# Attention and MoE block on one core: batches two to four in blocks of 256 and 320 rows, single-head score groups, spare products in a bank of their own

## The chip, the cores and the metric

The kernel runs on one core of a Trainium2 chip. The core has five engines with queues of their own: TensorE (PE, with its weight loads as PEld), VectorE (DVE), ScalarE (ACT), GpSimd (POOL) and SyncE (SP), which issues nearly all DMAs. The metric is device time in microseconds, as the median of several executions; a profiled execution gives the trace.

## The reference

Eight batches of eight heads go through attention whose weights are kept only near each row's maximum, and the result goes through a gated two-layer network. In short:

```
scores = q @ k.T / 8                                   # (8, 8, 576, 576), head size 64
keep   = scores >= rowmax(scores) - tau
attn   = exp(scores - rowmax) where keep, else 0
x      = (attn / (sum(attn) + 1e-9)) @ v               # heads side by side: (4608, 512)
h      = x @ w_in                                      # (4608, 2048)
out    = (h * sigmoid(h)) @ w_out                      # (4608, 512)
```

The weights `w_in` and `w_out` reach the kernel as 64-bit words.

## The kernel before, in words

**Visits.** The unit of attention is a visit: one pair of heads of one batch. Its rows are cut into tiles of 128 (numbers 0 to 3) and a tile 4 that holds the last 64 rows of both heads. `VISITS` names three kinds: "low" has tiles 0 and 1 (rows 0 to 255), "high" has tiles 2, 3 and 4 (320 rows), "all" has the five. Before, batch 0 is done as four low visits (0 to 3) and four high ones (4 to 7); batches 1 to 7 as four "all" visits each (8 to 35).

**A score group and its softmax.** For a tile of two heads, PE writes two score tiles `s` (there are two in all, pool "s") in one group that interleaves the heads (line 999). Then, per head: DVE takes the maximum (601) and the threshold (604), ACT the exponential (614), DVE masks and sums (621). Outside the low visits, the weights are split into two half-precision parts: ACT or POOL make the upper part (685, 687), POOL the lower (693, 694), and a DMA transposes both into a buffer `wT`. In the low visits ("direct") PE turns the weights in single precision (669) back into the score tile, and ACT copies them out (673).

**Dividing by the sum.** For batches below `UNDIVIDED` the weights stay undivided: the reciprocals are spread over the columns by PE (770), copied by ACT (835) and multiplied into the block on DVE (839, 844). From that batch on, ACT divides each tile's weights (636), after two tiny DVE instructions (628, 633).

**Query and key.** Each visit loads its pair's query and key (545), ACT gates the query (550), and, outside the low visits, ACT and POOL split both into two parts (561, 564).

**The network.** `moe(b, c0, n)` works on a block of n rows: 16 products groups `h` (891, 12 products each), tanh on ACT (898), two DVE instructions and an ACT copy (903, 908, 911), then 4 x 4 groups `o` (941), a copy out (953) and a store. Block (0,0), the first 256 rows of batch 0, is done in single precision (882, 933). Batches 1 to 7 are done in two blocks of 288 rows. A block needs the value products `a` (801, 809) of all four visits that cover its rows.

**The weights** are loaded in 32 chunks and rebuilt from their bits by ACT (401, 425), POOL (392, 428), DVE (404) and PE (417, for the maxima); later ACT and DVE split them (458, 461).

**What sets the order.** All operations are given to a planner (`Plan`) with a cost and a priority, most of them a place in the row of softmax tiles; tables such as `W_AT` and `Q_OFF` hold the places of weight chunks and loads. It lists them by its own costs, pool by pool, and the program is emitted in that order; each engine then runs its instructions strictly in it. PSUM holds the two `s` tiles and a pool of four banks ("bank") for everything else.

**Spare products.** `fill` puts products of no use (589) into gaps that the plan leaves on PE in its first 230 us, for 0.6 of each gap; `WARM` of them stand at the very start. Before, they write into the unused columns of the second bank of the score tile that was made last:

```
def products():
    for _ in range(n):
        nc.tensor.matmul(last_s[0][:, 1, 288:512], ones, wide, start=True, stop=True)
```

Of the kernel before, what the change touches and what calls it, by code (L numbers as in the profile page):

```python
# [20 lines left out]
P = 128  # L21
# [12 lines left out]
SEM = 50  # L34
# [17 lines left out]
class Plan:  # L52
# [134 lines left out]
    def fill(self, eng, until, least, each, make):  # L187

        end, out = 0.0, []
        for o in self.done:  # L190
            if o.eng == eng:
                n = int(FILL * (o.start - end) / each)
                if end < until and o.start - end > least and n > 0:
                    f = Op()
                    f.eng, f.occ, f.lat, f.name, f.fn, f.alloc, f.vs = eng, n * each, n * each, "fill", make(n), [], []
                    f.start, f.end, f.idx, f.prio, f.ready = end, end + n * each, o.idx, 0.0, 0.0
                    out.append(f)
                end = o.start + o.occ
        self.done = sorted(self.done + out, key=lambda o: (o.start, o.idx))
# [9 lines left out]
W_AT = (40.0, 24.01, 22.15, 61.37)  # L209
V_AT = 12.64  # L210
V_OFF = (-40.55, -32.27, -20.0, -3.3)
Q_OFF = (-7.69, -2.43, 1.82)
HIGH_AT = -3.91
W_STEP = (0.9, 0.83, 1.49, 0.77)
UNDIVIDED = 2
BIAS = 12 * math.log(2.0)
FILL = 0.6
FILL_UNTIL = 230.0e3
WARM = 60
# [10 lines left out]
def attention_moe(  # L230
# [48 lines left out]
    wide = ones[:, 0:1].to_broadcast([P, 224])  # L279
    ident = const.tile([P, P], F32, name="ident")  # L280
# [295 lines left out]
    last_s = [None]  # L576

    def new_s(nm):
        def make(slot):
            last_s[0] = ps_s.tile([P, 2, 512], F32, tag="s", name=f"s_{nm}")  # L580
            return last_s[0]

        return pl.value(f"s_{nm}", "s", make)

    def occupied(n):

        def products():
            for _ in range(n):
                nc.tensor.matmul(last_s[0][:, 1, 288:512], ones, wide, start=True, stop=True)  # L589

        return products

    def softmax(nm, u, v, parts, s, sums, direct=False):
# [59 lines left out]
        if direct:  # L653
            for h, i, r0, rows in parts:
                if (v, h) not in wT:
                    def make(slot, h=h):
                        full = sb.tile([P, 9, S], F16, tag="wT", name=f"wT_{v}_{h}", bufs=3)
                        full = full.rearrange("p j c -> p (j c)").bitcast(F32)[:, 0 : 5 * n]
                        return full.rearrange("p (j c) -> p j c", j=5)

                    wT[v, h] = pl.value(f"wT_{v}_{h}", "wT", make)
            ((h, i, r0, rows),) = parts
            out, c = wT[v, h], i * P - base

            def turned():
                flat = s.t.rearrange("p j c -> p (j c)")
                for k in range(5):
                    o = k * P if k < 4 else S - P
                    nc.tensor.transpose(flat[:, k * P : (k + 1) * P], w.t[:, o : o + P], ident)  # L669

            def kept():
                flat = s.t.rearrange("p j c -> p (j c)")
                nc.scalar.activation(
                    out.t[:, :, c : c + rows], flat[:, 0 : 5 * P].rearrange("p (k r) -> p k r", k=5), AF.Copy
                )
# [100 lines left out]
    def av(v, p, c0, n, u, rr):  # L776
# [3 lines left out]
        w2 = [wT[v, b * H + 2 * p + odd] for odd in range(2)]  # L780
        direct = kind == "low"
# [12 lines left out]
        def product():  # L794
            if rr is not None:
                spread(ps, c0, n, rr)
            if direct:
                for k in range(5):
                    r = slice(D, P) if k == 4 else slice(0, P)
                    for odd in range(2):  # L800
                        nc.tensor.matmul(
                            a.t[odd * D : (odd + 1) * D, :n], vt.t[r, odd, k, :], w2[odd].t[r, k, :],
                            start=(k == 0), stop=(k == 4),
                        )
                return
# [24 lines left out]
        op("PE", (3480 if direct else 1715 * k + 90) + more, (3650 if direct else 1715 * k + 260) + more, u - 500, product,  # L830
# [140 lines left out]
    warm = new_s("warm")  # L971
    op("PE", 9000, 9000, 10 * URGENT, occupied(WARM), [], [warm], name="warm")

# [4 lines left out]
    def visit(v, b, p, kind, u):  # L978
# [3 lines left out]
        direct = kind == "low"  # L982
# [20 lines left out]

        for i in tiles:
            if i < 4:
# [18 lines left out]
            cost = 1150 if direct else 1080 if i < 4 else 985  # L1024
            op("PE", cost, cost + 155, u, score, reads, ss, name=f"score{v}_{i}")
# [9 lines left out]
    for v, (b, p, kind) in enumerate(visits):  # L1035
        if p == 0 and b > 0:
            prepare_v(b, *((lambda p, o=o: u + 9 * p + o) for o in V_OFF[:2]), u + V_OFF[2],
                      lambda p: u + 9 * p + V_OFF[3])
        u = visit(v, b, p, kind, u + HIGH_AT) - HIGH_AT if kind == "high" else visit(v, b, p, kind, u)
        if p == NPAIR - 1:  # L1040
            if kind != "low":
# [3 lines left out]
            if kind == "low":  # L1045
# [4 lines left out]
    pl.fill("PE", FILL_UNTIL, 250.0, 95.0, occupied)  # L1050
# [50 lines left out]
```

## Time and profile before

| | us |
|---|---|
| median of 3 runs (1186.49 to 1189.03) | 1188.85 |
| profiled execution | 1183.31 |
| its span in the trace | 1181.4 |
| PE busy in the span | 1135.6 |
| DVE busy | 859.1 |
| ACT busy | 842.9 |
| POOL busy | 652.3 |
| first product of block (0,0), of (0,256), of batch 1's first block | 99.5, 201.2, 308.2 |
| last value product | about 1039 |

The span is the time between the first and last recorded instruction. A matmul's record reaches from its start to its result, so neighbours overlap, and a run of products is better read by the distance of their starts. A group of the page gives the source line, the engine, what is written and read, the count, busy time and the mean of one, and behind the second bar the idle time of the engine ahead of it and who ended that. In the waits view a line reads: who waited, for whom, total us, times, the longest.

### The profile page before, as it was taken

How to read it: one execution, taken by the hardware profiler on the slowest of the kernel's cores; microseconds unless marked ns; L12 is line 12 of the kernel's file. 1: busy time of each engine (PE TensorE's matmuls, PEld its weight loads, DVE VectorE, ACT ScalarE, POOL GpSimd, SP SyncE). 2: the span in 40 equal slices, each digit the busy share in tenths (PEclk: the TensorE clock that was granted, in tenths of full speed). 3: DMA queues.
4: the chain of work that ended last, by engine and by line, in shares of the span. 5: the costliest groups of instructions: out<-in, count | busy, mean ns of one | idle time of the engine just before them, and what ended most of it. 6: DMA issues, size and time to landing. Idle time of an engine off the chain costs nothing.

```text
span 1181.4 us, 27974 instructions
## 1 busy us (share of the span) xinstructions
PE 1135.6 (96%) x10212; PEld 893.8 (76%) x10212; DVE 859.1 (73%) x2412; ACT 842.9 (71%) x1529; POOL 652.3 (55%) x894
## 2 busy tenths in 40 slices
PE   8777899997899999999999999999999999999998
PEld 6555777775777777777777777777777777877777
DVE  4667899986887869687787878787887869541331
ACT  4776786875877878787887878787887878552341
POOL 0568798677667565666666465756666575400000
PEclk9999999999899999999999999999999999999999
DMA  8536577577677666775768576766766575600000
GB/s 328 165 115 166 113 176 173 108 123 151 120 121 144 109 135 125 132 139 110 136 117 151 103 140 116 141 109 128 136 120 127 95 135 95 107 6 21 11 11 21
DMA packets 352153, 141.17 MB, mean 119 GB/s; under 512 B 326416, under 2 KB 334608, under 8 KB 352016
## 3 DMA queue, kind: packets, MB, share of 16 engines
q1 hardware_dynamic: 352016, 139.38, 58.5%
q8 instruction: 81, 1.33, 0.5%
q14 instruction: 56, 0.46, 0.1%
HBM read 49.68 MB, written 9.44 MB: 50 GB/s over the span
## 4 chain that ended last, share of the span: by engine, by line
PE 83%; DVE 7%; POOL 4%; issue 3%; ACT 2%; DMA 2%; POOLq 0%; ACTq 0%; DVEq 0%
PE h L891 29%; PE o L941 29%; PE s L999 11%; PE a L809 9%; DVE w L621 2%; DMA wT<-hl 2%; PE s L589 2%; DVE sm L601 1%; POOL hl L693 1%; PE h L882 1%; PE s_warm L589 1%; PE s L669 1%; ACT w L614 1%; DVE wst L404 1%; POOL wst L428 0%
## 5 line engine op out<-in xcount | busy, mean ns | idle before, releaser
L941 PE MATMUL o<-gbuf,wst 128*128 128x288 f16 (+1 forms) x2880 | 371.2, 287 | 0.0
L891 PE MATMUL h<-x,wst 128*128 128x288 f16 (+1 forms) x2880 | 369.5, 287 | 0.4 <-DVE gbuf L911 0.4
L693 POOL TENSOR_TENSOR hl<-w,hl 128x512 f16<-128x512 f32 x272 | 321.0, 1180 | 84.1 <-ACT hl L685 73.3
L891 PEld LDWEIGHTS <-wst 128*128 128x128 f16 x2880 | 277.0, 98 | 80.2 <-issue 8.7
L941 PEld LDWEIGHTS <-wst 128*128 128x128 f16 x2880 | 275.8, 98 | 81.2 <-issue 10.4
L614 ACT ACTIVATE w<-s,sm 128x576 f32<-128x576 f32 x288 | 210.1, 739 | 76.3 <-DVE sm L601 45.1
L621 DVE SCALAR_TENSOR_TENSOR w<-s,sm,w 128x576 f32<-128x576 f32 x288 | 230.8, 814 | 45.5 <-ACT w L614 41.8
L601 DVE TENSOR_REDUCE sm<-s 128x1 f32<-128x576 f32 x288 | 208.3, 749 | 72.3 <-PE s L999 60.8
L687 POOL TENSOR_SCALAR hl<-w 128x576 f16<-128x576 f32 x136 | 91.7, 675 | 200.8 <-ACT w L636 167.1
L636 ACT ACTIVATE w<-w,sm 128x576 f32<-128x576 f32 x216 | 162.8, 772 | 53.4 <-DVE sm L633 31.0
L903 DVE SCALAR_TENSOR_TENSOR h<-th,h 128x288 f32<-128x288 f32 (+1 forms) x240 | 109.6, 458 | 69.2 <-ACT th L898 65.6
L898 ACT ACTIVATE th<-h,msc 128x288 f32<-128x288 f32 (+1 forms) x240 | 121.0, 504 | 21.6 <-PE h L891 19.1
L911 DVE SCALAR_TENSOR_TENSOR gbuf<-h,gbuf 128x288 f16<-128x288 f32 (+1 forms) x240 | 108.2, 454 | 36.5 <-ACT gbuf L908 36.1
L908 ACT ACTIVATE gbuf<-h 128x288 f16<-128x288 f32 (+1 forms) x240 | 97.8, 410 | 46.2 <-DVE h L903 45.6
L809 PE MATMUL a<-wT,v 128*64 128x288 f16 (+1 forms) x1680 | 110.7, 288 | 0.0
L685 ACT ACTIVATE hl<-w 128x576 f16<-128x576 f32 x136 | 92.5, 682 | 17.7 <-DMA wT<-hl 5.6
L809 PEld LDWEIGHTS <-v 128*64 128x64 f16 x1680 | 92.5, 110 | 13.3 <-issue 5.5
L999 PE MATMUL s<-khi,qhi 64*128 64x288 f32 (+1 forms) x544 | 88.2, 350 | 13.1 <-DVE w L621 12.6
L999 PEld LDWEIGHTS s<-khi,qhi 64*128 64x128 f32 (+1 forms) x544 | 49.9, 187 | 47.7 <-issue 42.5
L694 POOL TENSOR_TENSOR hl<-w,hl 128x64 f16<-128x64 f32 x272 | 85.7, 315 | 0.0
L953 ACT ACTIVATE ot<-o,msc 128x288 f32<-128x288 f32 (+1 forms) x60 | 29.7, 494 | 66.4 <-PE o L941 65.9
L999 PE MATMUL s<-klo,qhi 64*128 64x288 f32 (+1 forms) x544 | 67.9, 294 | 0.0
(95 smaller groups left out, 1172.8 us busy)
## 6 DMA issues: line engine op xcount, KB each, us to landing
qraw<-in_qT SPq DMA_DIRECT2D x36, 320.0 KB, 3.4
kraw<-in_kT SPq DMA_DIRECT2D x36, 288.0 KB, 3.0
vraw<-in_vL SPq DMA_DIRECT2D x32, 320.0 KB, 3.3
wst<-in_w_in SPq DMA_DIRECT2D x16, 512.0 KB, 6.4
out_t<-ot SPq DMA_DIRECT2D x56, 144.0 KB, 2.1
wT<-hl SPq DMA_TRANSPOSE x304, 3.3
wraw<-in_w_out SPq DMA_DIRECT2D x8, 512.0 KB, 4.7
wst<-in_w_out SPq DMA_DIRECT2D x8, 512.0 KB, 3.8
```

The costliest lines, as they stand in the source:

```text
L601: nc.vector.tensor_reduce(out=sm.t[:, 0:1], in_=s.t[:, :, :HALF], op=ALU.max, axis=AX.XY, negate=True)
L614: nc.scalar.activation(w.t.rearrange("p (j c) -> p j c", j=2), s.t[:, :, :HALF], AF.Exp, bias=sm.t[:, 0:1] if direct or sums is None else ...
L621: nc.vector.scalar_tensor_tensor(out=w3, in0=s.t[:, :, :HALF], scalar=sm.t[:, 1:2], in1=w3, op0=ALU.is_ge, op1=ALU.mult, accum_out=sm.t[:, ...
L636: nc.scalar.activation(w.t, w.t, AF.Copy, scale=sm.t[:, 5:6])
L693: nc.gpsimd.tensor_tensor(out=fl[:, 640:1152], in0=w.t[:, 0:512], in1=fl[:, 0:512], op=ALU.subtract)
L809: nc.tensor.matmul(a.t[odd * D : (odd + 1) * D, :n], vt.t[:, lo_v, odd, kv, :], w2[odd].t[:, kw, c0 - base : c0 - base + n], start=(k == 0 ...
L891: nc.tensor.matmul(ph.t[:, :n], wi(c, f, lo_w), xview(b, lo_x, c, c0, n), start=(j == 0), stop=(j == 11),)
L898: nc.scalar.activation(th.t[:, :n], ph.t[:, :n], AF.Tanh, scale=0.5 if whole else scale.t[:, 0:1])
L903: nc.vector.scalar_tensor_tensor(out=gwhole(g, n) if whole else ph.t[:, :n], in0=th.t[:, :n], scalar=1.0, in1=ph.t[:, :n], op0=ALU.add, op ...
L911: nc.vector.scalar_tensor_tensor(out=g.t[:, 1, :n], in0=ph.t[:, :n], scalar=2.0**-14, in1=g.t[:, 0, :n], op0=ALU.mult, op1=ALU.subtract,)
L941: nc.tensor.matmul(po.t[:, :n], wo(f, d, lo_w), gs[f].t[:, lo_g, :n], start=(f == 0 and j == 0), stop=(f == NF - 1 and j == 2),)
L999: nc.tensor.matmul(out[:, j, :HALF], q.t[rows, i * P : (i + 1) * P], k.t[rows, j * HALF : (j + 1) * HALF], start=(m == 0), stop=(m == len( ...
```

## The change

- `DIVIDED = 4`: batches 1 to 3 are also done as four low and four high visits, and their network in blocks of 256 and 320 rows. That makes 48 visits in place of 36: 0 to 7 are batch 0, 8 to 15 batch 1 (low, then high), 16 to 31 batches 2 and 3, and from 32 on "all" visits. Each visit loads, gates and splits its query and key, so 12 more of these. Only batch 0's low visits stay "direct".
- `UNDIVIDED = 1`: batch 1 divides its weights on ACT, and its spread reciprocals go.
- `SINGLE = 7`: in visits 0 to 6 each head of a 128-row tile has a score group and a place in the order of its own.
- In the low visits of batch 0 the two heads share one `wT` buffer (of three) where each had its own; their value product moves behind by `AV_AT`.
- Spare products write into a free bank of the pool of four, in the longest stretch of the gap in which one bank is free. `WARM` goes from 60 to 28. In the emitted program there are 100 in place of 348.
- An exponential of one column, right after the constant `ones` is set, makes ACT load its table at the start.
- All tables of places are set anew.

```diff
-    def fill(self, eng, until, least, each, make):
+    def fill(self, eng, until, least, each, pool, make):
...
+        def free(a, b):
+
+            best = (0.0, a, None)
+            for slot, uses in taken.items():
+                t = a
+                for start, stop in [*uses, (b, b)]:
+                    if stop >= a and t < b:
+                        best = max(best, (min(start, b) - t, t, slot), key=lambda q: q[0])
+                        t = max(t, stop)
+            return best
...
-W_AT = (40.0, 24.01, 22.15, 61.37)
+W_AT = (47.67, 22.01, 23.98, 99.13)
...
-UNDIVIDED = 2
+UNDIVIDED = 1
...
+SINGLE = 7
+DIVIDED = 4
+AV_AT = 13.6
...
-WARM = 60
+WARM = 28
...
+    table = const.tile([P, 1], F32, name="table")
+    nc.scalar.activation(table, ones[:, 0:1], AF.Exp)
...
     def occupied(n):
+
+        spare = bank("spare")

         def products():
             for _ in range(n):
-                nc.tensor.matmul(last_s[0][:, 1, 288:512], ones, wide, start=True, stop=True)
-
-        return products
+                nc.tensor.matmul(spare.t[:, 0:224], ones, wide, start=True, stop=True)
+
+        return products, spare
...
-        direct = kind == "low"
+        direct = kind == "low" and b == 0
...
-    visits = [(0, p, kind) for kind in ("low", "high") for p in range(NPAIR)]
-    visits += [(b, p, "all") for b in range(1, B) for p in range(NPAIR)]
...
+    visits = [
+        (b, p, kind) for b in range(B) for kind in (("low", "high") if b < DIVIDED else ("all",)) for p in range(NPAIR)
+    ]
...
         for i in tiles:
+            if i < 4 and v < SINGLE:
+                for r in range(2):
+                    s = new_s(f"{v}_{r}{i}")
+
+                    def score(s=s, i=i, r=r):
+                        for m in range(len(products)):
+                            for j in range(2):
+                                product(s.t, i, m, j, r)
+
+                    op("PE", cost(i), cost(i) + 155, u, score, reads, [s], name=f"score{v}_{r}{i}")
+                    softmax(f"{v}_{r}{i}", u, v, [(ha + r, i, 0, P)], s, sums, direct)
+                    u += 1
+                continue
```

Where it moves instructions. On PE, in the first visit, before (`s_0_00` is visit 0, head 0, tile 0; `s_0_10` the other head; `kraw`, `qraw` key and query):

```order
L589 MATMUL s_warm_129<-ones_80 128x224
L999 MATMUL s_0_00_224<-kraw_0_190,qraw_0_192 128x288
L999 MATMUL s_0_10_225<-kraw_0_190,qraw_0_192 128x288
L999 MATMUL s_0_00_224<-kraw_0_190,qraw_0_192 128x288
L999 MATMUL s_0_10_225<-kraw_0_190,qraw_0_192 128x288
L589 LDWEIGHTS ones_80
L589 MATMUL s_0_10_225<-ones_80 128x224
```

The heads stand interleaved, and the spare products behind them write into `s_0_10`. The same visit's second tile now (line 1022 is the score product, 691 the turn, 609 the spare products):

```order
L609 LDWEIGHTS ones_80
L609 MATMUL spare_232<-ones_80 128x224
L1022 MATMUL s_0_01_244<-kraw_0_160,qraw_0_162 128x288 x2
L691 MATMUL s_0_10_189<-ident_84,w32_0_10_221 128x128 x5
L609 LDWEIGHTS ones_80
L609 MATMUL spare_256<-ones_80 128x224
```

Head 0's scores of tile 1 stand ahead of head 1's turn of tile 0, and the spare products have a tile of their own. On ACT, at the end of batch 0's second block, before (`ot_0_256_3` is the copy out of that block's last columns; `w32_11_03` the exponential of visit 11, tile 3; `hl` a half copy; `khi`, `qhi` halves of key and query):

```order
L953 ACTIVATE ot_0_256_3_3860<-o_0_256_3_3580,msc_0_98 128x320
L614 ACTIVATE w32_11_03_3878<-s_11_03_3846,sm_11_03_3865 128x576
L614 ACTIVATE w32_11_13_3880<-s_11_13_3847,sm_11_13_3871 128x576
L685 ACTIVATE hl_11_03_3884<-w32_11_03_3878 128x576
L685 ACTIVATE hl_11_13_3895<-w32_11_13_3880 128x576
L561 ACTIVATE khi_13_3899<-kraw_13_3529 128x576
L561 ACTIVATE qhi_13_3902<-qraw_13_3550 128x640
```

Batch 1's first tanh stands 28 rows behind that copy. Now, around the same copy (line 975; 920 is the tanh, 930 the network's upper half, 659 the division, 838 the block's upper half):

```order
L920 ACTIVATE th_1_0_1_3561<-h_1_0_1_3509,msc_1_104 128x256
L659 ACTIVATE w32_14_04_3507<-w32_14_04_3507,sm_14_04_3501 128x576
L930 ACTIVATE gbuf_61<-h_1_0_1_3509 128x256
L838 ACTIVATE x16_1_2272<-a_1_1_256_3531 128x320
L535 ACTIVATE v16_2_1_3589<-vraw_2_1_2123,v2_s2_107 128x640
L637 ACTIVATE w32_15_02_3614<-s_15_02_3573,sm_15_02_3608 128x576
L975 ACTIVATE ot_0_256_3_3633<-o_0_256_3_3212,msc_0_100 128x320
```

Batch 1's second tanh now stands ahead of batch 0's last copy out; its first is 13 rows ahead.

More of the change, by code (lines that the diff above doesn't have):

```diff
@@ L185, in run @@
         return max(o.end for o in done)
-    def fill(self, eng, until, least, each, make):
+    def fill(self, eng, until, least, each, pool, make):
+        taken = {}
+        for o in self.done:
+            for x in o.alloc:
+                if x.pool == pool:
+                    taken.setdefault(x.slot, []).append((o.start, x.freed + SEM))
+        def free(a, b):
[7 more added lines that the diff above has]
+            return best
         end, out = 0.0, []
@@ L191, in fill @@
             if o.eng == eng:
[L192 to L197, printed above, removed]
+                if end < until and o.start - end > least:
+                    length, at, slot = free(end, o.start)
+                    n = int(FILL * length / each)
+                    if n > 0:
+                        f = Op()
+                        f.eng, f.occ, f.lat, f.name, f.deps = eng, n * each, n * each, "fill", set()
+                        f.fn, x = make(n)
+                        x.slot = slot
+                        f.alloc, f.vs = [x], [x]
+                        f.start, f.end, f.idx, f.prio, f.ready = at, at + n * each, o.idx, 0.0, 0.0
+                        out.append(f)
                 end = o.start + o.occ
@@ L653, in softmax, with make @@
         if direct:
[L654 to L661, printed above, removed]
-            ((h, i, r0, rows),) = parts
-            out, c = wT[v, h], i * P - base
+            ((h, i, r0, rows),) = parts
+            if v not in wT:
+                def make(slot):
+                    full = sb.tile([P, 9, S], F16, tag="wT", name=f"wT_{v}", bufs=3)
+                    full = full.rearrange("p j c -> p (j c)").bitcast(F32)[:, 0 : 10 * n]
+                    return full.rearrange("p (h j c) -> p h j c", h=2, j=5)
+                wT[v] = pl.value(f"wT_{v}", "wT", make)
+            out, c = wT[v], i * P - base
             def turned():
@@ L673, in kept @@
                 nc.scalar.activation(
-                    out.t[:, :, c : c + rows], flat[:, 0 : 5 * P].rearrange("p (k r) -> p k r", k=5), AF.Copy
+                    out.t[:, h % 2, :, c : c + rows], flat[:, 0 : 5 * P].rearrange("p (k r) -> p k r", k=5), AF.Copy
                 )
@@ L779, in av @@
         a = bank(f"a_{b}_{p}_{c0}")
-        w2 = [wT[v, b * H + 2 * p + odd] for odd in range(2)]
-        direct = kind == "low"
+        direct = kind == "low" and b == 0
+        w2 = [wT[v]] if direct else [wT[v, b * H + 2 * p + odd] for odd in range(2)]
         vt = VRAW[0, p] if direct else V16[b, p]
@@ L981, in visit @@
         tiles, ranges = VISITS[kind]
-        direct = kind == "low"
+        direct = kind == "low" and b == 0
         ha = b * H + 2 * p
@@ L1035, in attention_moe @@
     for v, (b, p, kind) in enumerate(visits):
-        if p == 0 and b > 0:
+        if p == 0 and b > 0 and b not in VS:
             prepare_v(b, *((lambda p, o=o: u + 9 * p + o) for o in V_OFF[:2]), u + V_OFF[2],
                       lambda p: u + 9 * p + V_OFF[3])
-        u = visit(v, b, p, kind, u + HIGH_AT) - HIGH_AT if kind == "high" else visit(v, b, p, kind, u)
+        at = HIGH_AT if kind == "high" and b == 0 else 0.0
+        u = visit(v, b, p, kind, u + at) - at
         if p == NPAIR - 1:
-            if kind != "low":
+            if b not in MSC and v >= NPAIR:
                 moe_scales(b, u - 4)
@@ L1044, in attention_moe @@
                 moe(b, c0, n)
-            if kind == "low":
+            if v < NPAIR:
                 split(0, W_AT[2], W_STEP[2])
```

33 lines of the change are left out of this document (15 added, 18 removed).

## Prediction

> **What bounds the kernel now.** I began with the page: how long each engine is busy, and the chain that ended last.
>
> ```profile
> span 1181.4 us, 27974 instructions
> PE 1135.6 (96%) x10212; PEld 893.8 (76%) x10212; DVE 859.1 (73%) x2412; ACT 842.9 (71%) x1529; POOL 652.3 (55%) x894
> PE 83%; DVE 7%; POOL 4%; issue 3%; ACT 2%; DMA 2%; POOLq 0%; ACTq 0%; DVEq 0%
> ```
>
> PE carries the chain, but a busy PE need not be a useful one. So second came the table of windows (per window: PE, PEld, DVE, ACT and POOL busy, then the granted clock), cut where block (0,0) starts, where PE gets dense, where batch 0's last block is nearly done, and where batch 1's first block starts; the row from 140 to 250 repeats the middle of the dense stretch.
>
> ```profile
> 0.00:99.50 99.50, 79.15 (x636) 58.75 (x636) 58.69 (x142) 65.34 (x103) 45.96 (x63) 0.97 0.61 207
> 99.50:130.00 30.50, 22.71 (x165) 18.68 (x166) 23.84 (x57) 19.70 (x35) 26.09 (x39) 1.00 0.53 102
> 130.00:280.00 150.00, 145.22 (x1218) 111.84 (x1216) 134.77 (x303) 112.32 (x203) 118.16 (x175) 1.00 0.71 146
> 280.00:308.20 28.20, 19.63 (x212) 15.60 (x210) 21.08 (x54) 17.01 (x27) 17.89 (x30) 0.76 0.70 134
> 140.00:250.00 110.00, 106.05 (x864) 82.45 (x861) 105.30 (x236) 87.15 (x160) 89.53 (x127) 1.00 0.73 150
> 308.20:1040.00 731.80, 730.85 (x6862) 578.91 (x6861) 578.04 (x1766) 580.16 (x1060) 444.24 (x591) 1.00 0.67 123
> ```
>
> From 308.2 on PE never rests. Up to 99.5 nothing is the bound: ACT is busy 66%, DVE 59%, and much of PE's 79 us are spare products. From 140 to 250 DVE is (105.30 of 110, 96%). The time is therefore **the moment at which batch 1's first block starts, plus the PE work behind it**.
>
> That work I count by paces: a block of 192 products and a visit's two value products from the chain in order of time, and from the PE timeline a score group, from its start to the next row's: two heads together, and tile 4, whose products go one after another.
>
> ```profile
> 338.62 3.55 PE a L809 x56
> ...
> 1060.46 23.52 PE o L941 x192
> 342.10 0.53 PE L999 MATMUL s<-khi,qhi 64*128 64x288 f32 x4
> ...
> 343.09 4.58 PE L941 MATMUL o<-gbuf,wst 128*128 128x288 f16 x36
> ...
> 351.45 0.53 PE L999 MATMUL s<-khi,qhi 128*128 128x288 f32 x2
> ...
> 352.35 0.91 PE L941 MATMUL o<-gbuf,wst 128*128 128x288 f16 x6
> ```
>
> A pair costs 0.99, tile 4 0.90. Behind 308.2 stand 28 runs of 192 (658.6), 93 pairs (92.1), 24 tiles 4 (21.6) and 23 visits' value products (81.7): 854. The rest of the span is 1181.4 - 308.2 = 873, so 19 us are not used there, tail included. In front of 308.2 lies the loss. Its last piece is the hole between the two batches, in the PE timeline:
>
> ```profile
> 286.49 0.54 PE L999 MATMUL s<-khi,qhi 64*128 64x288 f32 x4
> ...
> 291.12 0.82 PE L999 MATMUL s<-khi,qhi 128*128 128x288 f32 x2 [3.57 <-DVE w L621]
> ...
> 295.83 0.81 PE L999 MATMUL s<-khi,qhi 64*128 64x288 f32 x3 [2.39 <-DVE w L621]
> ...
> 300.05 0.58 PE L999 MATMUL s<-khi,qhi 64*128 64x288 f32 x1 [2.45 <-DVE w L621]
> ...
> 308.23 1.52 PE L891 MATMUL h<-x,wst 128*128 128x288 f16 x11
> ```
>
> For 22 us PE has only scores and value products, waiting for the masks of the tiles before them: batch 1's block needs all 36 softmax tiles of its batch. The first piece is the low visits. One of them, all engines:
>
> ```profile
> 40.12 2.10 PE L999 MATMUL s<-kraw,qraw 64*128 64x288 f32 x8
> ...
> 42.53 1.53 PE L589 MATMUL s<-ones 128*128 128x224 bf16 x14
> ...
> 44.09 0.76 DVE L601 TENSOR_REDUCE sm<-s 128x1 f32<-128x576 f32 x1 [1.18 <-PE s L589]
> ...
> 50.41 0.70 ACT L673 ACTIVATE wT<-s 128x640 f32<-128x640 f32 x1 [1.78 <-PE s L589]
> ```
>
> L589 are spare products, written into the second head's score tile. Its maximum waits 1.18 us for them, its copy out 1.78 us; the pair takes 10 us.
>
> **The change, part by part.** *Spare products in their own bank.* The waits on them sum up in the waits of the first 130 us, and in ACT's groups up to 99.5:
>
> ```profile
> DVE sm L601 <- PE s L589: 10.3, 10, 1.9
> L673 ACT ACTIVATE wT<-s 128x640 f32<-128x640 f32 x16 | 11.3, 704 | 10.6 <-PE s L589 5.9 <-PE s L669 2.7 <-DVE v_s L307 2.0
> ```
>
> 10.3 + 5.9 = 16.2 us go; some of it is covered by weight work that is then late instead, so I take three quarters, 12. Bounds: 0 and 16.2.
>
> *Table load and 28 first products.* Now ACT loads its table when the first query has landed, and the first score starts behind sixty products:
>
> ```profile
> 1.06 8.80 PE s_warm L589 x60
> 5.22 1.28 ACT L550 ACT_TABLE_LOAD   x1 [5.22 <-DMA qraw<-in_qT]
> ...
> 6.51 0.83 ACT L550 ACTIVATE qraw<-qraw,gate 128x640 f32<-128x640 f32 x1
> ...
> 9.79 1.36 PE L999 MATMUL s<-kraw,qraw 64*128 64x288 f32 x8
> ```
>
> The gated query can be ready at 5.22 + 0.83 = 6.1 instead of 7.3, and 28 products at 8.80 / 60 us, or somewhat slower at the start, end near 6.3. First score 3.4 us earlier. Bounds: 1 and 3.4.
>
> *Single-head groups.* A head's group starts when its own bank is free, and the two heads of a low visit share one weight buffer, so that three visits can be under way (no wait on it stands in the views: nothing). PE pays for it: in the three high visits six pairs of 0.99 become twice 0.90 (+4.9 us), in the low ones a pair takes 1.36 to 2.10 today and would take about 2.1 (0 to +6). PE has room for 5 to 11 us there. What the earlier maxima bring I can't price by a row; I count nothing, and keep it as the low end.
>
> *Stage 1, to block (0,0)'s first product.* The order puts 4 more exponentials, 5 more half copies and 5 fewer weight copies of ACT ahead of it: 65.3 + 4.5 = 70 us of ACT. So 99.5 - 3.4 - 12 + 4.5 = **88**, ACT at 80%. Bounds: 78 (ACT at 90%) and 104 (only the added work).
>
> *Stage 2, to batch 1's first product.* With 256 rows of each pair first, 16 tiles of batch 1 are needed instead of 36; the order has 12 maxima and 10 masks fewer ahead of that product, but 25 divisions on ACT more, since batch 1 now divides its weights:
>
> ```profile
> L621 DVE SCALAR_TENSOR_TENSOR w<-s,sm,w 128x576 f32<-128x576 f32 x288 | 230.8, 814 | 45.5 <-ACT w L614 41.8
> L601 DVE TENSOR_REDUCE sm<-s 128x1 f32<-128x576 f32 x288 | 208.3, 749 | 72.3 <-PE s L999 60.8
> L636 ACT ACTIVATE w<-w,sm 128x576 f32<-128x576 f32 x216 | 162.8, 772 | 53.4 <-DVE sm L633 31.0
> L550 ACT ACTIVATE qraw<-qraw,gate 128x640 f32<-128x640 f32 x36 | 29.8, 828 | 5.7 <-DMA qraw<-in_qT 5.0 <-POOL hl L687 0.2
> L561 ACT ACTIVATE qhi<-qraw 128x640 fp32r<-128x640 f32 x32 | 23.4, 733 | 0.0
> L561 ACT ACTIVATE khi<-kraw 128x576 fp32r<-128x576 f32 x32 | 21.7, 679 | 3.9 <-PE s L999 3.7
> L564 POOL TENSOR_TENSOR qlo<-qraw,qhi 128x640 fp32r<-128x640 f32 x32 | 49.5, 1547 | 1.4 <-ACT qhi L561 1.2
> ```
>
> DVE: 238.4 today (the first four windows) - 12 x 0.749 - 10 x 0.814 = 221; less stage 1's (58.7 and five maxima and masks, 66.5) leaves 155. ACT: 214.4 + 25 x 0.772 - 12 x 0.74 + two visits' query and key (0.828 + 0.733 + 0.679 = 2.24 each) = 229, less the half copies, reciprocal spreads and value copies that the order moves behind, about 218; less 70 leaves 148. PE's products there are those of 99.5 to 308.2, fewer scores. DVE held 90% from 130 to 280 and 96% at best, ACT 79% beside it. I take 166 us (DVE 93%, ACT 89%), nearer to DVE's rate, since DVE was the one that had no rest. Bounds: 155 (DVE without rest) and 187 (ACT at 79%). Batch 1's first product then starts at 88 + 166 = **254** (233 to 291).
>
> *Behind it.* The order leaves 28 runs, whose columns are the same (256 + 320 = 2 x 288), 98 pairs (97.0), 26 tiles 4 (23.4), 24 full visits' value products (85.2) and three 320-row ones (3 x 1.97): 870. I keep the 19 us and add 4, because ACT gets 12 x 2.24 = 27 us for the repeated query and key of twelve more visits: per batch PE works 94.1 + 33.6 = 127.7, three batches 383, ACT 0.793 x 383 + 27 = 331, or 86% instead of 79%. POOL (61% busy) takes a 1.55 and a shorter subtraction per visit, some 35 us; DMA repeats 24 loads at two thirds load. Both lie beside PE; without that cover they would cost up to those 35.
>
> Sum: 254 + 870 + 19 + 4 = 1147, against 1181.4. The profiled execution took 1183.31 with a span of 1181.4 (1.9 around it), and the median of the runs shown, 1188.85, is 5.5 above it: 1147 + 1.9 + 5.5 = **1154**.
>
> **The rivals.** *Stage 1 doesn't shrink* (17 in 100): the waits on spare products turn into waits on ACT's weight copies. For it: of ACT's 65 us in stage 1 the tiles take little more than a third, and weight chunks stand between them in its order. Then 104 + 166: 1147 + 16, and 1170. *The clock* (11): 248 spare products fewer. A turn of the PE timeline, and two windows:
>
> ```profile
> 23.54 0.98 PE L669 MATMUL s<-ident,w 128*128 128x128 f32 x5 [2.43 <-DVE w L621]
> 20.00:30.00 10.00, 7.49 (x56) 5.17 (x55) 5.30 (x18) 5.15 (x10) 1.61 (x4) 0.83 0.76 301
> 290.00:300.00 10.00, 4.09 (x18) 3.20 (x18) 8.00 (x18) 6.32 (x10) 7.12 (x11) 0.51 0.68 147
> ```
>
> With PE at 4 of 10 the clock was halved, at 7.5 of 10 partly. If it stays halved in the low visits, a head's score and turn grow by about 1.6 us, 16 heads in two banks: 13 us, so 1167. The Trainium skill (TensorE: Matmul & The Clock Gate, Part 1) says that an idle window of about 3.4 us halves the clock and as long a busy one restores it, which speaks against taking spare products away. By that rule single gaps under 3.4 us would do nothing. The window from 290 on, behind a gap of 3.57 us, agrees with it; the one from 20 on, with a gap of 2.43, does not, so the measured rows decide the price.
>
> *Slower* (9): ACT is the new bound. Place: stage 2 and batches 1 to 3; price: the extra divisions, queries and keys. If ACT cannot do more than share c of the time, stage 2 is 148/c and the three batches 331/c instead of 166 and 383. At c = 0.79, its rate from 140 to 250, that is 187 + 419: +57, and 1211. It decides below c = 0.82, where 479/c is 35 over 549. Against it: ACT's 79% came beside a full DVE, not as a limit.
>
> My forecast holds 60 in 100; its own range is 1135 to 1166. Three in 100 are left for terms that cancel. A change of 0.2% is about what can be told here: faster 0.88, within 0.03, slower 0.09. The range of 1131 to 1184 takes in both middle rivals and ends a little under the turning point.
>
> **What would show it.** Right: block (0,0) starts near 88, batch 1's first product near 254 and before batch 0's last output copy; no hole between batches; no maximum waiting for L609's spare products; ACT about 86 of 100 behind. Wrong: block (0,0) still near 100; clock under 0.9 up to 60 us; PE waiting for scores or key halves after 254.

## The result, and the profile after

The changed kernel takes 1154.24 us (1151.42 to 1155.25, four executions), the kernel before beside it 1187.67 (1185.26 to 1189.03): a ratio of 0.9717, with a 95% interval of 0.9692 to 0.9742. The forecast was 1154. Three of its terms missed, and cancelled; the runs below say which.

The page of the changed kernel: span, engines, the group of the maxima, and what was read from memory.

```profile
span 1151.9 us, 27405 instructions
PE 1123.0 (97%) x9868; PEld 875.6 (76%) x9868; DVE 862.5 (75%) x2468; ACT 878.2 (76%) x1599; POOL 677.8 (59%) x869
L624 DVE TENSOR_REDUCE sm<-s 128x1 f32<-128x576 f32 x288 | 209.6, 750 | 60.8 <-PE s L1022 59.8
HBM read 57.15 MB, written 9.44 MB: 58 GB/s over the span
```

Its windows, cut at the first product of block (0,0) (95.5) and of batch 1's first block (261.1); batches are counted from 0. The columns are as in the prediction: PE, PEld, DVE, ACT and POOL busy, the granted clock, the DMA share and GB/s.

```profile
0.00:95.50 95.50, 77.57 (x476) 53.21 (x476) 67.63 (x162) 69.05 (x111) 51.32 (x75) 0.82 0.64 207
95.50:261.10 165.60, 158.25 (x1230) 123.14 (x1230) 147.22 (x376) 142.89 (x256) 132.34 (x161) 0.99 0.73 157
261.10:1040.00 778.90, 778.63 (x7283) 612.76 (x7281) 618.13 (x1868) 631.03 (x1157) 494.16 (x633) 1.00 0.69 130
310.00:700.00 390.00, 389.73 (x3616) 302.26 (x3615) 316.26 (x963) 326.99 (x597) 260.84 (x328) 1.00 0.72 139
```

Stage 1 is 4.0 us shorter than before (95.5 against 99.5) and stage 2 is 43.1 shorter (165.6 against 208.7). Behind batch 1's first product lie 890.8 us against 873.2, since scores that used to stand ahead of that product now stand behind it. Together, -4.0 - 43.1 + 17.6 = -29.5 us, the whole difference of the two spans. (The medians differ by 33.4: the traced execution of the kernel before, 1183.31, is 4.4 us under its median, that of the changed kernel 0.4.) The repeated queries and keys show in what is read (57.15 MB, 49.68 before), and PE does not rest behind 261.1. Over the whole span the maxima's idle time fell from 72.3 to 60.8 us.

The hole between the batches is gone. The PE timeline where batch 0's last block (`o`, line 963) ends and batch 1's first (`h`, line 913) begins:

```profile
257.82 3.43 PE L963 MATMUL o<-gbuf,wst 128*128 128x320 f16 x24
261.09 1.47 PE L913 MATMUL h<-x,wst 128*128 128x256 f16 x12
...
263.19 1.81 PE L963 MATMUL o<-gbuf,wst 128*128 128x320 f16 x12
264.84 1.47 PE L913 MATMUL h<-x,wst 128*128 128x256 f16 x12
```

The two blocks run interleaved, with no row that carries an idle time. The last copy out of batch 0 starts at 271.10, ten us behind batch 1's first product.

In stage 1 the list of waits has no instruction of another engine that waits for the spare products. The largest waits of the first 95.5 us that touch the maxima, the copies out and the weight work:

```profile
POOL wst L455 <- PE wps L444: 21.0, 9, 8.8
DVE sm L624 <- PE s L1022: 11.4, 9, 2.8
ACT wT L695 <- PE s L691: 6.2, 7, 1.8
```

The maxima wait nearly as long as before, but for the scores themselves: 11.4 us, where in the first 99.5 us of the kernel before they waited 8.8 for spare products and 4.1 for scores. The clock bears on that, in three windows of the changed kernel:

```profile
28.20:31.60 3.40, 1.68 (x14) 0.94 (x11) 3.05 (x6) 3.00 (x6) 1.77 (x2) 1.00 0.54 171
31.60:35.00 3.40, 3.04 (x14) 2.37 (x12) 2.24 (x8) 2.38 (x5) 2.65 (x5) 0.52 0.74 219
35.00:55.60 20.60, 18.51 (x69) 12.26 (x68) 11.88 (x26) 13.99 (x23) 11.98 (x13) 0.50 0.50 158
```

After a stretch in which PE worked 1.68 of 3.40 us it ran at half speed for 24 us. In the PE timeline one head's scores take 2.28 us there and a turn 1.33, against 1.23 (at 11.73) and 0.77 at full clock, where the first two heads together take 1.25 (at 6.00); the longest idle time ahead of the halving is the 1.64 in front of 31.34. The rows:

```profile
6.00 1.25 PE L1022 MATMUL s<-kraw,qraw 64*128 64x288 f32 x8 [0.44 <-ACT qraw L577]
...
11.73 1.23 PE L1022 MATMUL s<-kraw,qraw 64*128 64x288 f32 x4 [0.21 <-ACT wT L695]
...
31.34 0.39 PE L444 MATMUL wps<-wst,ones 128*128 128x128 bf16 x4 [1.64 <-DVE wst L431]
...
42.69 1.33 PE L691 MATMUL s<-ident,w 128*128 128x128 f32 x5
43.95 2.28 PE L1022 MATMUL s<-kraw,qraw 64*128 64x288 f32 x4
...
67.24 0.77 PE L691 MATMUL s<-ident,w 128*128 128x128 f32 x5 [0.35 <-DVE w L644]
```

### The profile page after: what moved, and what is told of

It is laid out like the page before. It is cut to its first block, busy times and chain, and to the rows that moved or that the text cites. A ratio compares the mean times of both kernels' runs of the same rounds, so it can differ in the third digit from the quotient of the medians.

```text
span 1151.9 us, 27405 instructions
## 1 busy us (share of the span) xinstructions
PE 1123.0 (97%) x9868; PEld 875.6 (76%) x9868; DVE 862.5 (75%) x2468; ACT 878.2 (76%) x1599; POOL 677.8 (59%) x869
## 3 DMA queue, kind: packets, MB, share of 16 engines
HBM read 57.15 MB, written 9.44 MB: 58 GB/s over the span
## 5 line engine op out<-in xcount | busy, mean ns | idle before, releaser
L963 PE MATMUL o<-gbuf,wst 128*128 128x288 f16 (+2 forms) x2880 | 371.6, 287 | 0.0
L913 PE MATMUL h<-x,wst 128*128 128x288 f16 (+2 forms) x2880 | 370.3, 287 | 0.3 <-DVE gbuf L933 0.3
L624 DVE TENSOR_REDUCE sm<-s 128x1 f32<-128x576 f32 x288 | 209.6, 750 | 60.8 <-PE s L1022 59.8
L659 ACT ACTIVATE w<-w,sm 128x576 f32<-128x576 f32 x252 | 190.2, 775 | 55.9 <-DVE sm L656 41.4
L925 DVE SCALAR_TENSOR_TENSOR h<-th,h 128x288 f32<-128x288 f32 (+2 forms) x240 | 109.9, 458 | 63.0 <-ACT th L920 60.3
L933 DVE SCALAR_TENSOR_TENSOR gbuf<-h,gbuf 128x288 f16<-128x288 f32 (+2 forms) x240 | 108.4, 454 | 36.8 <-ACT gbuf L930 36.6
L920 ACT ACTIVATE th<-h,msc 128x288 f32<-128x288 f32 (+2 forms) x240 | 122.7, 511 | 13.0 <-PE h L913 11.0
L930 ACT ACTIVATE gbuf<-h 128x288 f16<-128x288 f32 (+2 forms) x240 | 99.5, 417 | 37.3 <-DVE h L925 36.7
L831 PE MATMUL a<-wT,v 128*64 128x288 f16 (+2 forms) x1680 | 112.3, 288 | 0.3 <-DVE gbuf L933 0.3
L975 ACT ACTIVATE ot<-o,msc 128x288 f32<-128x288 f32 (+2 forms) x60 | 29.9, 498 | 64.8 <-PE o L963 64.3
L591 POOL TENSOR_TENSOR qlo<-qraw,qhi 128x640 fp32r<-128x640 f32 x44 | 68.9, 1566 | 3.5 <-ACT qhi L588 2.3
```

Source lines behind the costliest of these rows:

```text
L624: nc.vector.tensor_reduce(out=sm.t[:, 0:1], in_=s.t[:, :, :HALF], op=ALU.max, axis=AX.XY, negate=True)
L659: nc.scalar.activation(w.t, w.t, AF.Copy, scale=sm.t[:, 5:6])
L831: nc.tensor.matmul(a.t[odd * D : (odd + 1) * D, :n], vt.t[:, lo_v, odd, kv, :], w2[odd].t[:, kw, c0 - base : c0 - base + n], start=(k == 0 ...
L913: nc.tensor.matmul(ph.t[:, :n], wi(c, f, lo_w), xview(b, lo_x, c, c0, n), start=(j == 0), stop=(j == 11),)
L920: nc.scalar.activation(th.t[:, :n], ph.t[:, :n], AF.Tanh, scale=0.5 if whole else scale.t[:, 0:1])
L925: nc.vector.scalar_tensor_tensor(out=gwhole(g, n) if whole else ph.t[:, :n], in0=th.t[:, :n], scalar=1.0, in1=ph.t[:, :n], op0=ALU.add, op ...
```

## The experiments

Twelve kernels were run, in three questions: what the division into 256 and 320 rows is worth, what the spare products and the clock are worth, and what is left for the rest. The texts of expectation count batches as the title does (the first is batch one), except in the words "batch 1's first block". The ratio compares each kernel with the kernel before as it ran beside it (medians of 1185.4 to 1187.7), so two times of the table can differ by some 2 us for that alone. The last three columns come from one traced execution each.

| kernel | time | ratio to before, 95% | block (0,0) | batch 1's first block | span behind that |
|---|---|---|---|---|---|
| before | 1187.67 | | 99.5 | 308.2 | 873.2 |
| changed | 1154.24 | 0.9717 (0.9692 to 0.9742) | 95.5 | 261.1 | 890.8 |
| changed, only batch 0 divided | 1171.70 | 0.9864 (0.9845 to 0.9883) | 95.7 | 298.5 | 871.5 |
| changed, batches 0 and 1 divided | 1167.35 | 0.9829 (0.9802 to 0.9856) | 91.7 | 259.8 | 905.8 |
| before, batches 0 to 3 divided, buffer shared | 1194.68 | 1.0058 (1.0041 to 1.0075) | 141.7 | 292.5 | 901.9 |
| changed, spare products in the score tile | 1156.98 | 0.9750 (0.9722 to 0.9778) | 101.8 | 268.8 | 891.1 |
| before, all batches divided | 1180.45 | 0.9937 (0.9922 to 0.9952) | 103.7 | 281.1 | 899.1 |
| before, spare products in a bank | 1172.11 | 0.9876 (0.9852 to 0.9899) | 85.8 | 294.9 | 874.5 |
| changed, more spare products | 1153.08 | 0.9705 (0.9691 to 0.9720) | 92.9 | 259.0 | 890.6 |
| changed, two-head groups | 1154.23 | 0.9715 (0.9699 to 0.9731) | 110.8 | 266.5 | 887.0 |
| before, bank, all batches divided | 1162.60 | 0.9801 (0.9780 to 0.9822) | 85.1 | 262.1 | 896.9 |
| changed, no spare products in gaps | 1166.80 | 0.9816 (0.9777 to 0.9855) | 105.5 | 272.3 | 895.0 |
| before, bank, batches 0 to 3 divided | 1166.00 | 0.9820 (0.9794 to 0.9846) | 85.0 | 264.6 | 901.4 |
| the same, batch 1 divides its weights | 1158.04 | 0.9755 (0.9733 to 0.9778) | 85.1 | 264.9 | 890.8 |

**Taking the division away again.** Two kernels undo it for batches 1 to 3, or for 2 and 3.

```diff
-DIVIDED = 4
+DIVIDED = 1
```

> The changed kernel, but batches two to four in undivided blocks of 288 rows again; all of the early part stays as changed. Theory A (the divided batches carry the gain: batch 1's first block needs 16 softmax tiles instead of 36, so the hole before it goes): block (0,0) still starts near 95 us, batch 1's first block starts near 300 instead of 261 with gaps of 2 to 4 us of PE before it, and the time is about 1176 (ratio 0.990). Rival B (the early part carries it: spare products in their own bank, single heads, earlier first score): the time stays near 1157 (0.975) and batch 1's first block starts before 275.

1171.7 us. Batch 1's first block starts at 298.5, and the hole is back, in the PE timeline and in its window:

```profile
275.56 0.58 PE L1022 MATMUL s<-khi,qhi 64*128 64x288 f32 x1 [4.78 <-DVE sm L627]
...
286.53 0.82 PE L1022 MATMUL s<-khi,qhi 64*128 64x288 f32 x3 [3.34 <-DVE w L644]
```

```profile
263.00:298.50 35.50, 20.49 (x195) 16.10 (x192) 23.59 (x77) 25.91 (x39) 22.56 (x32) 0.71 0.72 136
```

PE is busy 20.5 of 35.5 us there, much of it at half speed (clock 0.71). Theory A holds in place and size (17.5 us lost against 22 forecast). The start is 37 us later, yet the end only 17.5: the scores done in the hole are missing behind it (871.5 against 890.8).

```diff
-DIVIDED = 4
+DIVIDED = 2
```

> The changed kernel, but only batches one and two divided (256 + 320 rows); batches three and four in blocks of 288 rows. Theory A: only the division of the second batch matters, since PE is dense behind 261 us anyway; 18 us less of ACT and fewer loads change nothing that sets the end: 1150 to 1156 (0.968 to 0.973). Rival: the division of every batch keeps PE dense, and the two undivided batches give gaps of PE behind 400 us: 1160 to 1175.

1167.35 us: my theory fell and the rival held. The hole did not go, it moved to batch 2's first block (420.3), in the PE timeline and its window:

```profile
402.60 0.50 PE L1022 MATMUL s<-khi,qhi 128*128 128x288 f32 x2 [3.19 <-DVE sm L627]
...
407.26 0.82 PE L1022 MATMUL s<-khi,qhi 64*128 64x288 f32 x3 [3.24 <-DVE w L644]
```

```profile
398.00:420.30 22.30, 13.21 (x114) 10.12 (x111) 14.14 (x44) 16.53 (x26) 16.82 (x22) 0.69 0.67 136
```

An undivided batch needs 36 tiles before its first block, and the tiles are not that far ahead of PE so early. The division has to go on until they are.

**The division alone.** Three kernels add it to the kernel before. The first divides batches 0 to 3, as its text says.

```diff
+DIVIDED = 4
...
-    visits = [(0, p, kind) for kind in ("low", "high") for p in range(NPAIR)]
-    visits += [(b, p, "all") for b in range(1, B) for p in range(NPAIR)]
+    visits = [
+        (b, p, kind) for b in range(B) for kind in (("low", "high") if b < DIVIDED else ("all",)) for p in range(NPAIR)
+    ]
```

> The kernel before (its numbers of the order, sixty first products, spare products in the score tiles, two-head groups, no early table load), with only batches two to four also in blocks of 256 and 320 rows. Theory A: stage 1 as before (block (0,0) near 99), hole gone, batch 1's first block near 270: about 1163 (0.979). Rival B: the time stays at 1180 to 1190 (0.993 to 1.002), since the hole stays without the new early part.

1194.68 us, slower than before; block (0,0) starts at 141.7. This kernel was the changed one with its parts undone, and it kept one that I had overlooked: the two heads of a low visit share one `wT` buffer. So the division was run again as an edit of the kernel before, with a buffer per head, but now in all eight batches, though its text speaks of two to four (so does the text of the third kernel, further down, which also divides all eight).

```diff
-    visits = [(0, p, kind) for kind in ("low", "high") for p in range(NPAIR)]
-    visits += [(b, p, "all") for b in range(1, B) for p in range(NPAIR)]
+    visits = [(b, p, kind) for b in range(B) for kind in ("low", "high") for p in range(NPAIR)]
```

> The kernel before with nothing changed but that batches two to four too are computed in blocks of 256 and 320 rows (its own numbers of the order; the order up to block (0,0) is planned as before). Theory A (the division removes the hole by itself): block (0,0) near 99.5 as before, batch 1's first block near 266 (99.5 + the 166 of the changed kernel), about 893 behind it: time about 1163 (0.980). Rival C (it needs the other changes: with the old numbers new holes open at later blocks): batch 1's first block earlier than 308, but over 910 us behind it and a time of 1180 or more (0.994 or more).

1180.45 us, 7 us faster than before, with block (0,0) at 103.7. The two kernels lie 14 us apart, but they differ in two things, the shared buffer and the division of batches 4 to 7. Up to batch 1's first block, where both divide alike, the shared buffer goes with 11.4 us (292.5 against 281.1). Behind it the first kernel has a hole before batch 4's first block (710.9), the first that it does not divide; its window:

```profile
690.00:705.00 15.00, 8.76 (x69) 6.54 (x69) 11.13 (x37) 10.80 (x18) 12.01 (x16) 0.84 0.89 168
```

The second has no hole there (PE is busy 24.6 of the 24.6 us before its block at 684.6). So under the old numbers the shared buffer costs some 11 of the 14 us, an estimate; the changed kernel has the same buffer under new numbers. In the trace of the second, the division of all eight batches brings batch 1's first block 27 us forward and gives 26 us of it back behind (899.1 against 873.2); by the medians 7 are left. So rival C was nearer than theory A: without the other parts the division is worth a fifth of the change. The division of batches 1 to 3 alone, with a buffer per head and the old spare products, was not run.

**Spare products in a bank, alone.** The kernel before, with the new `fill` and `occupied` only.

```diff
-                nc.tensor.matmul(last_s[0][:, 1, 288:512], ones, wide, start=True, stop=True)
+                nc.tensor.matmul(spare.t[:, 0:224], ones, wide, start=True, stop=True)
```

> The kernel before with nothing changed but its spare products: into a free bank, 186 of them instead of 348, as the changed rule places them. My term (waits on spare products cost 12 us of stage 1, bounds 0 and 16): block (0,0) near 87, time about 1175 (0.990). Rival, the clock (fewer spare products let it halve in stage 1, as in the changed kernel from 32 to 56 us): block (0,0) near 95 to 100 with 20 us or more at half clock, time 1182 to 1190 (0.996 to 1.002). Third: waits turn into waits on weight copies: block (0,0) near 99 at full clock, same time.

1172.11 us: 15 us from this part. Block (0,0) comes 13.7 earlier; the clock in stage 1 is 0.94, so it did not fall as the rival had it. Its window and the waits of the maxima and copies out in it (lines 619 and 691 there):

```profile
0.00:85.80 85.80, 67.41 (x547) 49.91 (x547) 58.13 (x142) 64.55 (x103) 46.11 (x63) 0.94 0.70 240
```

```profile
ACT wT L691 <- PE s L687: 3.7, 7, 1.0
DVE sm L619 <- PE s L1017: 3.0, 3, 1.9
```

The 10.3 + 5.9 us of waits on spare products are gone and nothing of their size has taken their place. My term (12, bounds 0 and 16.2) was right for the kernel before. In the changed kernel it is worth less:

```diff
-    pl.fill("PE", FILL_UNTIL, 250.0, 95.0, "bank", occupied)
+    pl.fill("PE", FILL_UNTIL, 250.0, 95.0, occupied)
...
-                nc.tensor.matmul(spare.t[:, 0:224], ones, wide, start=True, stop=True)
+                nc.tensor.matmul(last_s[0][:, 1, 288:512], ones, wide, start=True, stop=True)
```

> The changed kernel with its spare products written into the free end of the last score tile again, 198 instead of 100 of them by the old rule; all else as changed. My term (the waits on spare products cost 12 us of stage 1): maxima and copies out wait for spare products again, block (0,0) starts near 107, the time is about 1166 (0.982). Rival (the clock): twice the spare products keep the clock full from 32 to 56 us, block (0,0) starts near 90, and the time is about 1149 (0.967). Third: both at once, within 3 us of 1154.

1156.98 us, so 2.7 us slower than the changed kernel; the two intervals overlap. Block (0,0) starts 6 us later in the traced execution (1161.65, 4.7 over the median), and the waits on spare products (line 593 there; of the first 130 us) are back, smaller than they were:

```profile
ACT w L618 <- PE s L593: 8.5, 6, 4.6
DVE sm L605 <- PE s L593: 4.1, 6, 1.1
```

It is the third outcome: waits and a fuller clock (198 products in place of 100; 0.87 up to block (0,0), where the changed kernel has 0.82) at once.

**The clock.** More spare products, and none:

```diff
-FILL = 0.6
+FILL = 1.5
```

> The changed kernel with FILL 1.5 instead of 0.6: 225 spare products instead of 100, in the same gaps. Theory, the clock: the window around 28 us gets over half busy, the clock stays full from 32 to 56 us, block (0,0) starts at 88 to 92 and the time is about 1149 (0.967). Rival (longer runs of spare products hold up scores and turns that are ready): block (0,0) at 95 or later, time 1154 to 1162 (0.972 to 0.979).

```diff
-FILL = 0.6
+FILL = 0.0
```

> The changed kernel with FILL 0: only the 28 first products are left, 72 spare products fewer in the low visits. Theory, the clock (a stretch of 3.4 us in which PE is busy less than half is followed by half speed): over 40 us at half clock before block (0,0), which starts at 100 to 108; because the part behind takes up only a part of a late block (0,0), the time is 1156 to 1163 (0.973 to 0.980). Rival (spare products are worth nothing now; the low visits wait for DVE and ACT): block (0,0) within 2 us of 95, time within 2 us of 1154.

Their first stages, and that of the kernel with batches 0 and 1 divided, whose order up to block (0,0) is the changed kernel's own on all five engines. One row of each, in this order:

```profile
0.00:92.90 92.90, 80.11 (x601) 60.28 (x601) 67.42 (x162) 68.37 (x111) 51.20 (x75) 0.94 0.66 213
```

```profile
0.00:105.50 105.50, 84.66 (x403) 55.25 (x403) 68.39 (x162) 69.79 (x111) 51.34 (x75) 0.64 0.60 188
```

```profile
0.00:91.70 91.70, 74.58 (x475) 51.78 (x475) 67.45 (x162) 68.87 (x111) 51.57 (x75) 0.87 0.67 216
```

A mean clock of 0.82 over 95.5 us is 2 x 0.18 x 95.5 = 34 us at half speed; the three rows give 11, 76 and 24 us. With the same instructions, 24 us in place of 34 bring block (0,0) at 91.7 in place of 95.5; with 72 spare products fewer, 76 us bring it at 105.5. That is 0.36 and 0.24 us of stage 1 for each us at half speed, and by these two the changed kernel's 34 us cost it some 8 to 12 (an estimate). The first row gives only 0.11 (92.9 with 11 us); there 125 more spare products stand in the way too, and the two effects were not separated.

The kernel before gives the price without such a change: of its 32 executions beside the twelve kernels the fastest took 1184.01 us at a mean clock of 0.991 and the slowest 1190.73 at 0.983, and a line through all 32 rises by 0.32 us for each us at half speed.

For the time: without spare products in the gaps 1166.8, 12.6 us more (four executions from 1159.47 to 1169.38), so 72 products that compute nothing are worth some 12. With 125 more, 1153.08: block (0,0) gains 2.6 us, and the time is not distinguishable from the changed kernel's. So the clock did what the theory of each text said, fuller with more products and half for 76 us without, but the times did not: 1153.08 where 1149 was expected, 1166.8 where 1156 to 1163 was.

By the Trainium skill (TensorE: Matmul & The Clock Gate, Part 1) an idle window of some 3.4 us halves the clock, and as long a busy one restores it. The length of the stretches agrees (3.4 us and its multiples), the conditions do not: the halving at 31.6 came after a stretch whose longest idle time was 1.64 us, and 18.5 busy us of 20.6 did not end it. The row from 290 on, which the prediction took for agreement, is no better: in the kernel before half speed began at 290.19, 2.6 us into the gap of 3.57 that ended at 291.12, behind a stretch with 0.78 us of products:

```profile
286.78:290.19 3.41, 0.78 (x12) 0.54 (x10) 1.97 (x6) 1.16 (x3) 2.59 (x5) 1.00 0.93 184
```

**Two-head groups.**

```diff
-SINGLE = 7
+SINGLE = 0
```

> The changed kernel with SINGLE 0: score groups of two heads in all visits, as before; 158 spare products by the same rule. What I counted for single heads is nothing beside 5 to 11 us of PE: then block (0,0) starts within 3 us of 95 and the time is within 4 us of 1154 (0.968 to 0.975). Rival (the single heads are what keeps three visits under way in stage 1): block (0,0) at 103 to 112, time 1161 to 1172 (0.978 to 0.987).

1154.23 us, no difference, as the first text had it, and yet block (0,0) starts at 110.8, as the rival had it. Its two stages:

```profile
0.00:110.80 110.80, 82.12 (x627) 61.07 (x628) 80.10 (x189) 81.89 (x132) 72.56 (x101) 0.85 0.66 209
110.80:266.50 155.70, 151.14 (x1173) 117.15 (x1171) 138.35 (x365) 132.99 (x238) 120.52 (x151) 1.00 0.74 155
```

DVE and ACT did 12 to 13 us more before the block than in the changed kernel (80.1 and 81.9 against 67.6 and 69.1) and 9 to 10 us less behind it. An order that starts the block later but works ahead on the next tiles loses nothing: the start of block (0,0) is not what sets the end.

**Putting it together.** The last three kernels add parts to the kernel before.

> The kernel before with two parts of the change together: the spare products in a free bank (186 of them) and batches two to four divided; its own numbers of the order, two-head groups, no early table load. If the parts add up (-15.4 and -7.1 us alone): 1165 (0.981). If they are the whole change, and single heads, table and new numbers are worth nothing: 1154 (0.972), batch 1's first block near 262. If both take the same loss away: 1172 or more (0.987), with losses behind batch 1's first block as in the kernel with the division alone.

1162.6 us: bank and division (of all eight batches) nearly add up.

```diff
+    visits = [(b, p, kind) for b in range(B)
+              for kind in (("low", "high") if b < 4 else ("all",)) for p in range(NPAIR)]
```

> The kernel before with the spare products in a free bank and, as in the change, batches two to four divided and batches five to eight in blocks of 288 (the three earlier kernels that added the division to the kernel before divided all eight batches). If dividing batches five to eight cost the 6 us that stood behind batch 1's first block (897 against 891): 1157 (0.975). If the end of the divided batches opens a hole before the first block of the fifth, as it did before the third where only two were divided: a gap of 10 us or more of PE between 500 and 620 us, and 1168 to 1175 (0.985 to 0.990).

1166.0 us. The hole opens, as the second text had it, before the first undivided batch's block, only later than I wrote, 666 to 682.6, and with a time 2 us under its range. (The text is wrong on one of the earlier kernels: the one with the shared buffer divided batches 0 to 3, and has its hole at the same batch.) In the PE timeline and its window:

```profile
670.34 0.50 PE L1016 MATMUL s<-khi,qhi 64*128 64x288 f32 x3 [2.72 <-DVE w L639]
...
674.22 0.58 PE L1016 MATMUL s<-khi,qhi 64*128 64x288 f32 x1 [2.85 <-DVE w L639]
```

```profile
666.00:682.60 16.60, 10.61 (x102) 8.23 (x100) 10.82 (x37) 12.36 (x19) 13.13 (x18) 0.79 0.91 156
```

```diff
-UNDIVIDED = 2
+UNDIVIDED = 1
```

> As the last one, and the second batch divides its weights on ScalarE too (UNDIVIDED 1): what is then left of the change are single heads, the early table load with 28 first products, the shared buffer of a visit and the new numbers of the order. PE has some 80 spread products less (2 us); ACT has up to 36 divisions of 0.775 us more ahead of batch 1's last blocks. If ACT has room: 2 to 4 us faster than the last one, 1153 to 1155 if that took 1157. If my worry (ACT as the new bound of stage 2) holds: batch 1's first block 5 us or more later than without, and slower by as much.

1158.04 us, 8 us faster. Batch 1's first block starts where it did (264.9), so ACT has the room, and the hole at 670 is gone, which the text had not foreseen (it gave 2 to 4 us). Its windows:

```profile
85.10:264.90 179.80, 164.15 (x1254) 125.96 (x1255) 155.01 (x396) 144.75 (x258) 140.65 (x181) 0.96 0.71 145
264.90:1040.00 775.10, 772.85 (x7240) 608.31 (x7238) 612.99 (x1869) 630.69 (x1155) 493.21 (x636) 1.00 0.69 129
```

PE loses 2.3 us of those 775, where the kernel without this line lost 7.3 (768.08 of 775.40), and does 80 spread products less. Why the tiles are further ahead with this line was not separated: it gives ACT more work and the order changes with it.

**Where the time was.** If every product but the spare ones is counted at its own pace at full clock (a 288-column one at 23.52 / 192 us, a pair of scores at 0.99, a single head's at half of its pair's, and so on, so that what single heads cost PE counts as lost), 1055 to 1057 us of each span are useful; the rest is lost, by stretch:

| kernel | 0-100 | 100-200 | 200-310 | 310-500 | 500-700 | 700-1040 | from 1040 | all |
|---|---|---|---|---|---|---|---|---|
| before | 64.9 | 23.7 | 18.0 | 4.9 | 4.1 | 5.0 | 3.3 | 124.0 |
| + bank | 57.9 | 19.0 | 16.5 | 4.4 | 5.5 | 5.4 | 3.4 | 111.9 |
| + batches 0 to 3 divided | 58.1 | 19.0 | 3.6 | 5.4 | 14.0 | 4.9 | 3.4 | 108.6 |
| + batch 1 divides its weights | 58.1 | 19.4 | 2.8 | 5.0 | 4.9 | 6.6 | 3.4 | 100.3 |
| changed | 59.4 | 15.2 | 3.7 | 5.0 | 5.0 | 4.7 | 3.4 | 96.5 |
| changed, two-head groups | 63.4 | 14.3 | 3.1 | 5.6 | 3.6 | 4.8 | 3.4 | 98.1 |

Of the 33 us of the change the bank gives 15, the division of batches 1 to 3 some 6, batch 1's own division of its weights 8, and single heads, shared buffer, early table load, 28 first products and new numbers together the last 4 (1158.0 to 1154.2, hardly more than the intervals tell). The order of adding matters: taken away from the changed kernel, the division costs 17.5 us and the bank 2.7. More spare products gave the lowest time, 1153.08, but not one that can be told from the changed kernel's.

## Why the prediction was right, and where it was not

**What bounds.** Right: PE is dense behind batch 1's first product, and the loss in front of it was to be had. What fell is the use of that moment as a clock. Taking the division away moved it by 37 us and the end by 17.5, and two-head groups moved block (0,0) by 15 us and the end by nothing. My sum survived this because it counted the moved scores on both sides of the mark.

**Spare products in their own bank, -12.** The mechanism was right, and the size for the kernel before (13.7 us at block (0,0), the waits gone). In the changed kernel the part is worth 2.7 us, and even that is not clear of the intervals.

**First score, -3.4.** It starts at 6.00 in place of 9.79, 3.8 earlier. What that brings to the end was not run by itself.

**Single heads, nothing.** Right for the time (1154.23 without them), though without them block (0,0) starts 15 us later, which I had not seen. The shared buffer, which I put at nothing with them, costs some 11 us under the old numbers; what it costs in the changed kernel was not run.

**Stage 1, 88: the step that failed.** It measured 95.5 (the terms as written add up to 88.6). The sum took the clock of the kernel before (0.97) for granted; it fell to 0.82, at a price of some 8 to 12 us by the estimate above: the mechanism of the rival that I gave 11 in 100 and 13 us. Up to 60 us the clock was 0.80, one of my own signs of being wrong. Nor was ACT the limit of this stage: its work was as summed (69.1 us against 70), but it was busy 72% of 95.5 and not 80% of 88. The other rival (104, by waits on ACT's weight copies) was as far off in number, and the waits on ACT in the list are small: 3.1 us of the masks for exponentials, 3.0 of DVE's weight work and 1.2 of the scores for copies out. That the clock is the whole of the 7.5 us was not shown; other waits, above all the maxima's for the scores, were not priced.

**Stage 2, 166.** It measured 165.6, by two errors that met: DVE had 147 us of work there and not 155, ACT 143 and not 148, and they were busy 89 and 86 of 100, not 93 and 89.

**Behind it, 893.** 890.8. ACT is busy 327 of 390 us between 310 and 700, 84% (86 forecast), and PE waits for nothing there: the added queries and keys lie beside it, as costed. *Slower, ACT as the new bound* is refuted by the kernel in which batch 1's division was added: more work for ACT, 8 us less.

**The change as a whole.** I took `UNDIVIDED = 1` for a cost of 25 divisions with nothing in return; under the old numbers it closes a hole that the division of batches 1 to 3 merely moves. That a hole can move to the first undivided batch was in none of my cases.

**The offset.** I added 7.4 us between span and median; it was 2.3 (1154.24 - 1151.9). The 5.5 in it came from a traced execution of the kernel before that took 1183.31 at a mean clock of 0.991, quicker than all 32 named above, which start at 1184.01 (the middle one of their clocks is 0.987); by 0.32 us for each us at half speed, the clock alone makes some 3 of the 5.5 (an estimate). Stage 1 7.5 late, the part behind 2.2 and the offset 5.1 less: the exact hit is a sum that cancels, the sign and size are not.

## What to carry to other kernels

A bubble at a boundary is removed only when the producers' lead has caught up with what the next piece needs; make the first pieces small until then, and look for the bubble where the small pieces end. Products that only keep PE busy should write where nobody waits, and before some of them are cut, count how many stretches fall under half busy. A milestone in the middle of a kernel is a witness, not a clock: compare what was lost up to a time, not when one block starts.

## What was not expected of the hardware

In the fourteen traces of these kernels the clock's changes lie 3.41 us apart or a multiple of it. Cut into such stretches, the first 150 us and those from 270 to 310 show 70 changes to half speed, three quarters of them behind stretches in which PE was busy less than half the time and none above 0.72 (by its matmul records, whose ends are modelled), and 70 changes back, all behind stretches busy at least 0.86. Full speed outlived five stretches under half busy (the lowest 0.44), and half speed outlived some that were busy throughout, so busy time alone does not decide it; whether the kind of product counts was not separated. In these traces full speed was lost behind stretches up to 0.72 busy and won back only behind 0.86 and more, and it varies between executions: two kernels with the same order up to block (0,0) spent 34 and 24 us of it at half speed.
